# Moving eight weight sums of a fused attention and MLP kernel from GpSimd to VectorE

## The chip, the cores and the metric

One core of one Trainium2 chip. The metric is the device time of one execution in microseconds; times below are medians of all runs. A single core's run counts as slow when it is over 1.5% above the fastest of the same kernel, and ratios and means use fast runs alone; the slow ones are named where they fall. A ratio is the mean time of one kernel's fast runs over the mean of the other's fast runs in the same rounds, so it is not quite the ratio of the medians quoted beside it.

Engine names in the profile: PE is TensorE's matmuls, PEld its weight loads, DVE is VectorE, ACT is ScalarE, POOL is GpSimd. "L276" is line 276 of the kernel's file. The granted clock is the share of TensorE's full clock that its throttle let through. An eviction is the VectorE or ScalarE instruction that empties a PSUM bank. A V group is a run of 28 matmuls of the sigmoid scores with v.

## The reference, cut to what matters

```python
# q, k, v: (8, 12, 448, 64); w_in: (768, 2048); w_out: (2048, 768); all float32
scores = q @ k.T / sqrt(64) - log(448)
attn   = sigmoid(scores) @ v                # no softmax: a plain sigmoid
x      = attn, heads side by side: (3584, 768)
h      = x @ w_in
out    = (h * sigmoid(h)) @ w_out
```

The kernel works in float16 and multiplies by w_out with a Strassen-like scheme: w_out and the activations are cut into quarters, seven products replace eight, and sums of quarters are needed on both sides.

## The kernel before

Everything is put in order on the host by a planner (`Plan`), which models when each engine is free and emits each instruction when its time comes. On the chip the engines run their queues in that order and wait for each other by semaphores.

Loads are issued from GpSimd's queue:

```python
def load(key, deps, fn, nd, size):
    first = [("issue", pl.loads)] if pl.loads else []
    pl.loads += 1
    pl.op("POOL", 650, key, deps + first, fn, nbytes=...)
```

Elementwise operations go to VectorE (`tt`) or GpSimd (`tt_pool`). The quarter sums of w_out are made once, in two halves of four sums each, 1536 columns a sum, all on GpSimd:

```python
def tt(key, dur, deps, o, a, b_, op, prio=0):
    pl.op("DVE", dur, key, deps, lambda: nc.vector.tensor_tensor(o, a, b_, op), prio=prio)      # L276

def tt_pool(key, n, deps, o, a, b_, op, prio=0):
    pl.op("POOL", 100 + 2.2 * n, key, deps, lambda: nc.gpsimd.tensor_tensor(o, a, b_, op), prio=prio)  # L279

def sums_wo(f0, f1):                                # called for (0, 4) and (4, 8)
    ...
    for z, (o, x_, y_) in enumerate(((t1, a12, a11), (t2, a22, t1), (a12, a22, a12), (t4, a21, t2))):
        dz = dep if z == 0 else [kk + (z - 1,)]
        if z in (0,1,2,3):
            tt_pool(kk + (z,), (f1 - f0) * HE, dz, o, x_, y_, sub, 5)
        else:
            tt(kk + (z,), d, dz, o, x_, y_, sub, 5)
```

The matching sums of the activations, 1024 columns each and four for each of 14 row blocks, are on VectorE. They all go through `tt`, so the profile has them at line 276:

```python
# G2.sums
tt(kk + (1,), 600, self.deps + old(0), s1, a21, a22, add, -1)
tt(kk + (2,), 600, [kk + (1,)] + old(1), s2, s1, a11, sub, -1)
tt(kk + (3,), 600, [kk + (2,), kk + (1,)], a21, a11, a21, sub, -1)
tt(kk + (4,), 600, [kk + (2,)] + old(2), s4, a12, s2, sub, -1)
```

VectorE also empties PSUM. The silu multiply (line 624 of the kernel before) reads a PSUM bank and the sigmoid that ScalarE made of it, and frees the bank:

```python
pl.op("ACT", 50 + ncol / 1.2, key + ("sg",), dep,
      lambda: nc.scalar.activation(t[:, :ncol], src_, AF.Sigmoid, scale=ISX), prio=0)
pl.op("DVE", 65 + ncol / 0.96, key + ("g",), [key + ("sg",)] + list(guard),
      lambda: nc.vector.tensor_tensor(o, src_..., t[:, :ncol]..., ALU.mult))
```

There are eight banks, and TensorE stops when all of them wait to be emptied.

## Time and profile before

| | kernel before |
|---|---|
| time, median of 3 runs | 400.0 us (399.7 to 401.24) |
| TensorE busy | 94% of the span |
| VectorE, ScalarE, GpSimd busy | 53%, 58%, 23% |
| GpSimd's eight sums | 25.1 us |

TensorE is the bound. In a kernel like this the thing to read is not the busy shares but the few places where TensorE is not busy, or busy at a lower clock: the row of 40 slices shows where, the list of waits shows for whom, and the timeline of the engine that was waited for shows why. The prediction below prints those lines, and they are not repeated here.

### The profile page before, as it was taken

The numbers are of one execution on the slowest core, as the hardware profiler recorded it, in microseconds if no ns is written. First come the engines' busy times: TensorE is split into PE (matmuls) and PEld (weight loads), VectorE is DVE, ScalarE is ACT, GpSimd is POOL, SyncE is SP. The second block draws the span as 40 slices with busy tenths as digits, with TensorE's granted clock in tenths as the row PEclk, the third lists the DMA queues.
The fourth block names the chain that finished last, engine by engine and source line by source line (L and its number), as shares of the span: only waits on it lengthen the run. The fifth ranks groups of instructions, "written<-read, shape, count | busy, mean of one in ns | idle before, by whom it ended". The sixth has DMA issues, their size and how long they took to land.

```text
span 400.2 us, 17994 instructions
## 1 busy us (share of the span) xinstructions
PE 375.7 (94%) x8024; PEld 315.7 (79%) x8024; DVE 211.1 (53%) x368; ACT 232.8 (58%) x506; POOL 90.1 (23%) x105
## 2 busy tenths in 40 slices
PE   7999869995999999969999999999999999999995
PEld 3676757893887889958898889887989888988773
DVE  4536694797326447415365254554554545554633
ACT  2994629625787686445955697658647766134110
POOL 9656461892222202202022012220200000000000
PEclk9999968997999999998999999999999999999998
DMA  8999990990599996866688999988875101310235
GB/s 111 200 209 203 211 167 2 139 146 2 72 143 196 214 169 104 118 148 121 71 137 107 185 148 130 140 127 116 131 125 115 24 2 43 82 44 2 52 73 120
DMA packets 80636, 46.51 MB, mean 116 GB/s; under 512 B 50608, under 2 KB 79792, under 8 KB 80560
## 3 DMA queue, kind: packets, MB, share of 16 engines
q0 software_dynamic: 25008, 22.81, 38.4%
q1 hardware_dynamic: 55552, 22.56, 33.7%
q8 instruction: 63, 1.03, 1.0%
q14 instruction: 13, 0.11, 0.1%
HBM read 45.61 MB, written 11.01 MB: 141 GB/s over the span
## 4 chain that ended last, share of the span: by engine, by line
PE 82%; DMA 6%; DVE 5%; ACT 3%; issue 2%; POOL 0%; ACTq 0%; DVEq 0%; POOLq 0%
PE ps L803 31%; PE ps L677 29%; PE ps L502 8%; PE ps L514 8%; PE ps L713 5%; DMA xk<-in_k_dram 5%; DVE gs L276 2%; ACT at L952 2%; DVE gt L624 1%; DMA xq<-in_q_dram 1%; PE ps L985 1%; ACT sg L619 1%; PE ps L460 1%; DVE kT L474 1%; ACT at L545 0%
## 5 line engine op out<-in xcount | busy, mean ns | idle before, releaser
L677 PE MATMUL ps<-xt,wi 64*64 64x448 f16 x2304 | 166.9, 352 | 4.1 <-issue 3.7
L545 ACT ACTIVATE at<-ps 128x448 f16<-128x448 f32 x252 | 122.3, 553 | 50.8 <-PE ps L502 43.3
L677 PEld LDWEIGHTS <-wi 64*64 64x64 f16 x2304 | 114.7, 108 | 17.4 <-issue 6.1
L624 DVE TENSOR_TENSOR gt<-ps,sg 128x448 f16<-128x448 f32 (+2 forms) x128 | 78.0, 621 | 76.6 <-ACT sg L619 76.5
L803 PE MATMUL ps<-wo,gt 64*64 64x384 f16 x1344 | 114.9, 326 | 3.3 <-DVE gt L624 3.3
L803 PEld LDWEIGHTS <-gt 64*64 64x64 f16 x1792 | 98.9, 108 | 15.6 <-issue 5.9
L619 ACT ACTIVATE sg<-ps 128x448 f16<-128x448 f32 (+2 forms) x128 | 69.8, 552 | 63.9 <-PE ps L677 32.6
L803 PEld LDWEIGHTS <-gs 64*64 64x64 f16 x1344 | 78.9, 108 | 8.8 <-issue 0.7
L803 PE MATMUL ps<-so,gs 64*64 64x384 f16 x896 | 83.0, 326 | 0.0
L502 PE MATMUL ps<-qT,kT 64*64 64x448 f16 (+2 forms) x840 | 80.4, 334 | 2.2 <-DVE gt L624 1.1
L817 DVE SCALAR_TENSOR_TENSOR us<-ps,us 128x384 f32<-128x384 f32 x70 | 38.8, 555 | 56.7 <-PE ps L803 46.7
L239 POOL DMA_DIRECT2D v<-in_v_dram x24 | 17.4, 724 | 194.2 <-PE ps L514 77.8
L502 PEld LDWEIGHTS <-kT 64*64 64x64 f16 x840 | 37.5, 112 | 12.7 <-issue 8.1
L952 ACT ACTIVATE at<-ps 128x512 f16<-128x512 f32 (+3 forms) x96 | 39.6, 543 | 10.8 <-PE ps L502 10.7
L803 PE MATMUL ps<-so,gt 64*64 64x384 f16 x448 | 44.6, 323 | 0.1
L514 PE MATMUL ps<-at,v 64*64 64x448 f16 (+2 forms) x840 | 42.1, 322 | 2.7 <-DMA xk<-in_k_dram 1.5
L713 PE MATMUL ps<-xt,wi 128*128 128x256 f16 (+1 forms) x384 | 42.8, 268 | 1.4 <-issue 1.1
L803 PE MATMUL ps<-wo,gs 64*64 64x384 f16 x448 | 43.7, 323 | 0.0
L713 PEld LDWEIGHTS <-wi 128*128 128x128 f16 x384 | 34.8, 101 | 6.6 <-issue 2.8
L514 PEld LDWEIGHTS <-v 64*64 64x64 f16 x840 | 30.9, 110 | 7.3 <-issue 3.6
L824 ACT ACTIVATE us<-ps 128x384 f32<-128x384 f32 x28 | 14.0, 501 | 30.3 <-PE ps L803 30.3
L557 DVE TENSOR_SCALAR xt<-ps 128x448 f16<-128x448 f32 x36 | 20.9, 619 | 17.8 <-PE ps L514 16.2
(33 smaller groups left out, 183.8 us busy)
## 6 DMA issues: line engine op xcount, KB each, us to landing
out_dram<-us SPq DMA_DIRECT2D x112, 96.0 KB, 3.1
xk<-in_k_dram POOLq DMA_DIRECT2D x24, 224.0 KB, 6.2
v<-in_v_dram POOLq DMA_DIRECT2D x24, 224.0 KB, 5.2
xq<-in_q_dram POOLq DMA_DIRECT2D x21, 224.0 KB, 7.3
wo<-in_moe_w_out_dram POOLq DMA_DIRECT2D x4, 768.0 KB, 15.3
wi<-in_moe_w_in_dram POOLq DMA_DIRECT2D x8, 192.0 KB, 7.1
wi<-in_moe_w_in_dram POOLq DMA_DIRECT2D x4, 384.0 KB, 9.5
qT<-xq SPq DMA_TRANSPOSE x32, 4.7
```

What stands on the lines that cost most here:

```text
L239: lambda: nc.gpsimd.dma_start(v16[n % NV], src(v, b, g)),
L502: nc.tensor.matmul(pt[r][64 * h : 64 * h + 64, lo : lo + (c1 - c0) * D], kT[n % NTR][64 * r : 64 * r + 64, i, 64 * h : 64 * h + 64], qT[n ...
L514: nc.tensor.matmul(pt[h][64 * j : 64 * j + 64, :N], v16[n % NV][64 * h : 64 * h + 64, j, c * D : (c + 1) * D], at[64 * h : 64 * h + 64, sl ...
L545: lambda r=r: nc.scalar.activation(at[:, sl, r], pt[r][:, :S], AF.Sigmoid, bias=NEG_LOG_S, scale=QKSCALE),
L557: lambda h=h: nc.vector.tensor_scalar_mul(x[:, 2 * g + h, :], pt[h][:, :S], SX), prio=-2,
L619: lambda: nc.scalar.activation(t[:, :ncol], src_, AF.Sigmoid, scale=ISX), prio=0,
L624: lambda: nc.vector.tensor_tensor(o, src_.rearrange("p (a t) -> p a t", a=nb), t[:, :ncol].rearrange("p (a t) -> p a t", a=nb), ALU.mult),
L677: nc.tensor.matmul(bank[64 * j : 64 * j + 64, z * N : z * N + N], wi[64 * h : 64 * h + 64, cc, f0 + 64 * j : f0 + 64 * j + 64], x[64 * h : ...
L713: nc.tensor.matmul(bank[:, z * N : z * N + N], wi[:, cc, fc * P : (fc + 1) * P], x[:, cc, self.c0 : self.c1], start=(cc == 0 and z == 0), ...
L803: nc.tensor.matmul(bank[64 * j : 64 * j + 64, :HE], lhs[64 * h : 64 * h + 64, c, 64 * j : 64 * j + 64], rhs[64 * h : 64 * h + 64, c, :], s ...
L817: lambda: nc.vector.scalar_tensor_tensor(o, bank[:, :HE], ISX, u, ALU.mult, ALU.add), prio=-2,
L952: lambda r=r, src_=src_: nc.scalar.activation(at[:, base : base + m, r, :N], src_, AF.Sigmoid, bias=NEG_LOG_S, scale=QKSCALE),
```

## The change

The intent: give the eight w_out sums to VectorE, which has room on average, and keep everything else.

```diff
+    last_load = [None]
     def load(key, deps, fn, nd, size):
         first = [("issue", pl.loads)] if pl.loads else []
+        if key[0] in ("k", "q", "v") and key[1] >= 99:
+            first.append(last_load[0])
+        last_load[0] = key
...
-            if z in (0,1,2,3):
+            if z in ():
                 tt_pool(kk + (z,), (f1 - f0) * HE, dz, o, x_, y_, sub, 5)
             else:
                 tt(kk + (z,), d, dz, o, x_, y_, sub, 5)
```

The edit of `load` has no effect, because attention groups are numbered 0 to 23. All lines from there on move down by five: 276 becomes 281, 624 becomes 629, 803 becomes 808.

## The prediction

> **What bounds the kernel now.** I read the page's busy shares and its 40 slices first, then what TensorE (PE) waits for, then the VectorE (DVE) and GpSimd (POOL) timelines around the two slices where PE drops. From the page's first two parts:
>
> ```profile
> PE 375.7 (94%) x8024; PEld 315.7 (79%) x8024; DVE 211.1 (53%) x368; ACT 232.8 (58%) x506; POOL 90.1 (23%) x105
> ...
> PE   7999869995999999969999999999999999999995
> ...
> PEclk9999968997999999998999999999999999999998
> ```
>
> PE is 94% busy, so only its holes and its slow-clock stretches can be won. One slice is 10 us. Holes stand in slices 50-60, 90-100 and 170-180 us, and the granted clock falls in or right after each. The waits of PE between 30 and 110 us name the first two (columns: engine, line, what it waited for, us in total, times, longest):
>
> ```profile
> PE ps L803 <- DVE gt L624: 3.3, 1, 3.3
> PE ps L460 <- DVE gt L624: 2.3, 1, 2.3
> PE ps L514 <- DMA xk<-in_k_dram: 1.5, 1, 1.5
> PE ps L502 <- DVE gt L624: 1.1, 2, 0.6
> ```
>
> Line 624 is the silu multiply on VectorE that empties a PSUM bank. Why is it late, when VectorE is only 53% busy? Its timeline and GpSimd's (start, duration, engine, line):
>
> ```profile
> 47.92 1.57 DVE L276 TENSOR_TENSOR gs<-gt 128x1024 f16<-128x1024 f16 x1
> ...
> 49.87 3.44 DVE L276 TENSOR_TENSOR gs<-gs,gt 128x1024 f16<-128x1024 f16 x1
> ...
> 53.71 3.11 DVE L276 TENSOR_TENSOR gt<-gt 128x1024 f16<-128x1024 f16 x1
> 56.74 0.68 DVE L276 TENSOR_TENSOR gs<-gt,gs 128x1024 f16<-128x1024 f16 x1
> ...
> 83.72 9.30 DVE L276 TENSOR_TENSOR gs<-gt 128x1024 f16<-128x1024 f16 x1
> ```
>
> ```profile
> 45.85 3.08 POOL L279 TENSOR_TENSOR so<-wo 128x1536 f16<-128x1536 f16 x1 [4.81 <-DMA wo<-in_moe_w_out_dram]
> 49.68 3.09 POOL L279 TENSOR_TENSOR so<-wo,so 128x1536 f16<-128x1536 f16 x1 [0.75 <-DMA wo<-in_moe_w_out_dram]
> 52.72 3.54 POOL L279 TENSOR_TENSOR wo<-wo 128x1536 f16<-128x1536 f16 x1
> ...
> 80.24 6.16 POOL L279 TENSOR_TENSOR so<-wo,so 128x1536 f16<-128x1536 f16 x2
> 86.35 3.09 POOL L279 TENSOR_TENSOR wo<-wo 128x1536 f16<-128x1536 f16 x1
> 89.39 3.07 POOL L279 TENSOR_TENSOR so<-wo,so 128x1536 f16<-128x1536 f16 x1
> ```
>
> The same VectorE sum takes 0.68 us or up to 9.30 us. Every long one ends about 0.56 us after a GpSimd sum ends: GpSimd 48.93, VectorE 49.49; 52.77 and 53.31; 56.26 and 56.82; 92.46 and 93.02. So the long durations are blocking, not work. In the last case VectorE was passed over by four GpSimd sums in a row.
>
> The 1.5 us put down to a DMA I read differently. That matmul (57.94) writes a bank which the program order makes wait for a line 624 multiply, and that multiply ends at 57.88. It is the same stall.
>
> **What the Trainium skill says.** "SBUF — State Buffer", section "Who interferes with whom": a VectorE instruction with two SBUF inputs contends with a GpSimd instruction that reads SBUF, and the later one blocks for the whole instruction. The pairs above agree. "VectorE: DVE Perf Modes", the errata section, gives (N+151)/0.96 ns for a two-input op; the tier table gives such ops 2x on 16-bit data. With N/2 for N = 1024 that is 690 ns; the trace has 676 to 693 ns unblocked. "GPSIMD Engine Reference", section 4.1, calls GpSimd about 2x slower for two inputs. This trace has 3.09 us per 1536 columns there against my 0.96 us below, so 3.2x. "TensorE: Matmul & The Clock Gate", Part 1: about 3.4 us of idleness halves the clock. After the holes the trace has 0.67 (50-60 us) and 0.72 (90-100 us), and matmuls of 192 columns in groups of twelve take 2.10 instead of 1.16 us.
>
> **The change, part by part.**
>
> Removed: eight GpSimd sums, 4 x 3095 + 2 x 3314 + 2 x 3094 ns = 25.1 us. GpSimd is 23% busy, so that time itself is worth nothing.
>
> Removed with it: the VectorE blocking. First stall (1.57 + 3.44 + 3.11) - 3 x 0.68 = 6.1 us; second 9.30 - 0.68 = 8.6 us. Together 14.7 us of VectorE.
>
> Added: eight VectorE sums of 1536 columns. Estimate from the skill's form above, whose slope the trace confirms: (768+151)/0.96 = 957 ns, so 7.7 us in all. VectorE's net load falls by 7 us.
>
> Moved: the built program has the same 16,050 rows on PE, in another order from row 2169 on (the host-side planner sees other times). The eight sums sit in VectorE's queue among the multiplies and evictions: six between about the 60 and 69 us positions of the old trace, one each later. The load edit tests for a number of 99 or more; attention groups are numbered 0 to 23, so it does nothing.
>
> Worth on PE, first stall. I redo the VectorE chain by hand with 0.68 us sums. The sum of 49.87 then ends near 50.3, the multiply waiting on ScalarE (ACT) runs 51.5-52.0, two sums end near 53.3, the next multiply near 53.8. So the matmul group of 57.94 starts near 53.9: 4.1 us won, and PE idles about 0.7 instead of 3.8 us, too little for the clock to fall. The slow clock after the old stall (about 2.6 us from 57.94 to 63) mostly stays hidden: ScalarE is 9.05 of 10 us busy in 60-70 and runs one queue of evictions from 60.15 to 67.9. I count 0.8 us of it. So 4.9 us before the new work. Then four of the added sums come before the evictions that the matmuls of old time 66.40 need. By the same chain the eviction comes near 62.4, where ScalarE would have let PE start near 61.2: minus 1.2 us. **Net first stall: about 3.7 us.**
>
> Second stall. PE idles 3.35 + 0.55 + 0.54 = 4.4 us (its timeline at 93.55, 94.61 and 95.68). From 93.55 to 101.0 it is at half rate: four matmuls start per 0.33 us where 0.165 is normal later. That is 7.45 - 1.09 of waits = 6.4 us at half rate, so 3.2 us lost. Before it PE is 10.00 of 10 us busy (80-90), and after it 10.00 of 10 (100-110), so nothing else hides this gain. **Second stall: about 7.6 us.**
>
> Sum 11.3 us; 400.0 - 11.3 = 388.7. I take **389 us**.
>
> **The rivals.**
>
> 1. VectorE becomes the bound where the six sums crowd. Between 60 and 70 us it has 4.1 us of work, and six sums add 5.7 us into an interval that itself shrinks: nearly full, with in-order evictions behind 1 to 2 us of sums. For it: these are the stages where PE borrows banks from evictions. Against: the old VectorE sat idle 2.1, 1.6, 1.9 and 1.2 us there, and the planner places the sums at lowest priority. If it bites fully, the first stall gives back all its 3.7 us and the result is 392 to 393.
>
> 2. The hole is hidden anyway: ScalarE or the w_out and K/V loads pace 45-70 us. For it: DMA runs near 210 GB/s until 58 us and ScalarE's 9.05 of 10. Against: all weight pieces lie in SBUF before VectorE reaches the sums (GpSimd saw the first two at 45.85 and 49.68; they leave at about 3.8 us each, so the last comes near 57.5, and VectorE needs it near 63). This costs only the first stall again.
>
> 3. The later program is another order with other luck. One hole at 175.64 lasts 3.06 us with every engine idle and no releaser ("issue"), and runs cold for some us after. I do not know its cause; if it is an accident of timing it may vanish (minus 4 us) or another may come (plus 4 us).
>
> 4. GpSimd's loads starve behind VectorE sums, since it must write descriptors. The skill's page infers that two-input ops spare the write side. Loads are far ahead of use after 60 us, so I give it 1 us at most.
>
> **Range and chances.** Both stalls are plain in the trace and their cause ends the moment GpSimd stops reading SBUF; that gives 11.3 us as centre. Rival 1 takes up to 4, rival 3 is plus or minus 4, and a fuller recovery of the slow clock in the first stall gives up to 2 more. So 383 to 394. Faster by 2% needs under 392.0: it fails only if rival 1 bites fully or a new hole comes, 0.79. Within 2% 0.20, slower 0.01.
>
> **What would show it.** Right: line 276 sums all near 0.68 us, with none over 1.2; eight new sums near 0.96 us each; no PE wait on line 624 over 1 us between 80 and 100 us and no fall of the clock there; VectorE busy down by about 7 us to near 204; PE busy down by 4 to 6 us to near 370, as cold matmuls vanish; GpSimd busy near 65. Wrong: PE waits on VectorE of 1 to 3 us between 55 and 75 us (rival 1); unchanged evictions but holes marked issue or DMA elsewhere (rival 3); sums that still last over 1.2 us, which would mean the blocker was the GpSimd DMA issues and not its sums.

## The result, and the profile after

| | before | after |
|---|---|---|
| median | 400.62 us (4 runs, 399.7 to 403.27) | 385.81 us (4 runs, 385.25 to 387.09) |
| ratio of fast runs | | 0.9624, 95% interval 0.957 to 0.9679 |

It is faster by 3.8%, 14.8 us by the medians. The predicted time was 389 us and the predicted gain 11.3 us.

The page of the kernel after, busy shares, then TensorE's row of slices and its granted clock (one slice is now 9.6 us):

```profile
PE 366.5 (95%) x8024; PEld 307.8 (80%) x8024; DVE 203.5 (53%) x376; ACT 232.6 (60%) x506; POOL 65.1 (17%) x97
...
PE   7899899999998899989999999999999999999994
...
PEclk9999999999999999999999999999999999999998
```

The 6 and the 5 of the two holes are gone, and the clock stays in the top tenth in every slice but the last. TensorE's busy time fell by 9.2 us for the same 8024 matmuls. That fits matmuls that had run at a lower clock: a group of twelve that took 2.10 us in the first stall takes 1.16 or 1.17 us now.

What TensorE waited for between 30 and 110 us in the kernel after (line, what for, us in total, times, longest):

```profile
PE ps L718 <- issue: 1.1, 1, 1.1
PE ps L507 <- issue: 0.4, 1, 0.4
PE ps L507 <- ACT at L957: 0.3, 1, 0.3
```

No wait for VectorE is left. VectorE's timeline after (start, duration, engine, line, operation), with the sums that correspond to those of 1.57, 3.44, 3.11 and 9.30 us before:

```profile
47.35 0.68 DVE L281 TENSOR_TENSOR gs<-gt 128x1024 f16<-128x1024 f16 x1
...
48.41 0.68 DVE L281 TENSOR_TENSOR gs<-gs,gt 128x1024 f16<-128x1024 f16 x1
...
49.48 0.68 DVE L281 TENSOR_TENSOR gt<-gt 128x1024 f16<-128x1024 f16 x1
...
54.47 0.95 DVE L281 TENSOR_TENSOR so<-wo 128x1536 f16<-128x1536 f16 x1
55.45 0.96 DVE L281 TENSOR_TENSOR so<-wo,so 128x1536 f16<-128x1536 f16 x1
...
76.71 0.69 DVE L281 TENSOR_TENSOR gs<-gt 128x1024 f16<-128x1024 f16 x1
```

Each old sum takes its own 0.68 to 0.69 us, and the new ones 0.95 us. Two stretches of the two kernels side by side, first before and then after. The columns are the stretch in us, its length, the busy time of PE, PEld, DVE, ACT and POOL with instruction counts, the granted clock, the DMA share and GB/s:

```profile
50.00:60.00 10.00, 6.20 (x99) 5.32 (x100) 10.00 (x10) 2.98 (x8) 6.26 (x2) 0.67 0.96 169
90.00:100.00 10.00, 5.56 (x48) 3.24 (x49) 7.95 (x11) 5.12 (x11) 2.47 (x1) 0.72 0.01 2
```

```profile
50.00:60.00 10.00, 9.40 (x199) 7.32 (x196) 9.68 (x19) 8.77 (x23) 0.00 (x0) 1.00 1.00 176
90.00:100.00 10.00, 10.00 (x236) 8.47 (x230) 3.52 (x6) 8.33 (x20) 2.15 (x3) 1.00 1.05 164
```

VectorE is 10.00 us "busy" before with 10 instructions and 9.68 us after with 19. A blocked instruction counts as busy, which is why the shares alone did not give the stall away.

Where the time came from can be read off by following the same pieces of work through both TensorE timelines:

| piece of TensorE's work | before, us | after, us | lead |
|---|---|---|---|
| V group ahead of the first stall | 46.25 | 45.68 | 0.57 |
| V group held up in the first stall | 57.94 | 52.31 | 5.63 |
| first w_in matmuls of the second batch | 66.40 | 59.77 | 6.63 |
| run of 132 w_in matmuls begins | 78.18 | 71.16 | 7.02 |
| first product with w_out | 93.55 | 83.12 | 10.43 |
| first V group of 448 columns | 105.24 | 90.50 | 14.74 |
| end | 400.2 | 384.5 | 15.7 |

The first row is scatter between executions, since nothing differs up to there. The first stall gives 7.02 - 0.57 = 6.45 us, the second 14.74 - 7.02 = 7.72 us, and the 295 us after it 1.0 us. That last 1.0 us is a net of larger terms, which no part of the change was meant to give: the 2000th matmul starts 15.1 us earlier than before (at 117.2 us before), the 3000th only 11.2 us (163.6) and the 4000th again 14.7 us (213.3). Short holes in TensorE's work took the time, and an older hole that is gone gave it back (see rival 3 below). That they nearly cancel is luck.

One reading of the page could now be checked. The wait of the matmuls of 57.94 had been put down to the landing of a K load, 19.0 us after its issue at 39.15. That is near 58.2, after they had started. In the kernel after that load takes 18.9 us from 39.88 and lands near 58.8, long after the same matmuls have started at 52.31. They never needed it.

### The profile page after: what moved, and what is told of

Its sections match the earlier page's. It is cut to its first block, busy times and chain, and to the rows that moved or that the text cites. A ratio compares the mean times of both kernels' runs of the same rounds, so it can differ in the third digit from the quotient of the medians.

```text
span 384.5 us, 17994 instructions
## 1 busy us (share of the span) xinstructions
PE 366.5 (95%) x8024; PEld 307.8 (80%) x8024; DVE 203.5 (53%) x376; ACT 232.6 (60%) x506; POOL 65.1 (17%) x97
## 4 chain that ended last, share of the span: by engine, by line
PE 90%; issue 3%; ACT 2%; DMA 2%; POOL 1%; DVE 1%; POOLq 0%; ACTq 0%
PE ps L808 33%; PE ps L682 30%; PE ps L718 10%; PE ps L507 8%; PE ps L519 8%; ACT at L957 2%; DMA xk<-in_k_dram 2%; PE ps L465 1%; PE ps L990 1%; POOL xk L224 0%; POOL xq L233 0%; DVE qT L479 0%; DVE xt L979 0%; ACT sg L624 0%; POOL v L244 0%
## 5 line engine op out<-in xcount | busy, mean ns | idle before, releaser
L682 PEld LDWEIGHTS <-wi 64*64 64x64 f16 x2304 | 112.6, 107 | 19.3 <-issue 7.0
L808 PE MATMUL ps<-wo,gt 64*64 64x384 f16 x1344 | 111.5, 323 | 0.3 <-issue 0.3
L808 PEld LDWEIGHTS <-gt 64*64 64x64 f16 x1792 | 97.8, 107 | 10.7 <-issue 1.9
L808 PE MATMUL ps<-so,gs 64*64 64x384 f16 x896 | 80.6, 323 | 0.0
L507 PE MATMUL ps<-qT,kT 64*64 64x448 f16 (+2 forms) x840 | 76.5, 318 | 2.2 <-ACT at L957 0.9
L507 PEld LDWEIGHTS <-kT 64*64 64x64 f16 x840 | 35.7, 108 | 11.9 <-issue 7.8
L718 PE MATMUL ps<-xt,wi 128*128 128x256 f16 (+1 forms) x384 | 40.8, 260 | 1.1 <-issue 1.1
L519 PE MATMUL ps<-at,v 64*64 64x448 f16 (+2 forms) x840 | 40.9, 313 | 0.6 <-issue 0.6
L718 PEld LDWEIGHTS <-wi 128*128 128x128 f16 x384 | 33.1, 98 | 5.8 <-issue 2.5
L519 PEld LDWEIGHTS <-v 64*64 64x64 f16 x840 | 29.8, 107 | 6.2 <-issue 2.2
```

The lines of the kernel that those rows point to most:

```text
L507: nc.tensor.matmul(pt[r][64 * h : 64 * h + 64, lo : lo + (c1 - c0) * D], kT[n % NTR][64 * r : 64 * r + 64, i, 64 * h : 64 * h + 64], qT[n ...
L519: nc.tensor.matmul(pt[h][64 * j : 64 * j + 64, :N], v16[n % NV][64 * h : 64 * h + 64, j, c * D : (c + 1) * D], at[64 * h : 64 * h + 64, sl ...
L682: nc.tensor.matmul(bank[64 * j : 64 * j + 64, z * N : z * N + N], wi[64 * h : 64 * h + 64, cc, f0 + 64 * j : f0 + 64 * j + 64], x[64 * h : ...
L718: nc.tensor.matmul(bank[:, z * N : z * N + N], wi[:, cc, fc * P : (fc + 1) * P], x[:, cc, self.c0 : self.c1], start=(cc == 0 and z == 0), ...
L808: nc.tensor.matmul(bank[64 * j : 64 * j + 64, :HE], lhs[64 * h : 64 * h + 64, c, 64 * j : 64 * j + 64], rhs[64 * h : 64 * h + 64, c, :], s ...
```

## The experiments

The theory: a GpSimd operation that reads SBUF blocks a VectorE operation with two SBUF inputs, and the VectorE queue behind it holds PSUM banks. Rivals: the planner's new program order made the gain; GpSimd's sums or the loads queued behind them came too late; any GpSimd work on SBUF blocks. All kernels gave correct results, on two chips: e1 to e4 on one and the rest on another. "Before" is the kernel before, run beside them. All runs were fast but one of e5's four (397.91 us) and one of the kernel before in each of the two later batches (408.39 and 406.19 us).

| run | what it does | median, us | ratio to before (95%) |
|---|---|---|---|
| e1_order_before | sums on VectorE, TensorE's order of before | 383.93 | 0.959 (0.954 to 0.964) |
| e2_order_after | sums on GpSimd, TensorE's order of after | 395.27 | 0.985 (0.980 to 0.991) |
| e3_dummy_read | e1 plus eight useless GpSimd subtractions | 405.56 | 1.010 (1.005 to 1.016) |
| e4_dummy_write | e1 plus sixteen useless GpSimd memsets | 384.92 | 0.960 (0.956 to 0.964) |
| e5_first_on_gpsimd | only the first half's sums on GpSimd | 394.54 | 0.980 (0.970 to 0.989) |
| e6_second_on_gpsimd | only the second half's sums on GpSimd | 393.03 | 0.980 (0.974 to 0.986) |
| e7_sums_apart | all on GpSimd, VectorE's sums moved away | 386.89 | 0.964 (0.956 to 0.973) |
| e8_after_beside | the kernel after | 388.57 | 0.969 (0.962 to 0.975) |
| f1_order_before | e1 again | 387.10 | 0.968 (0.964 to 0.972) |
| f2_after | the kernel after again | 386.00 | 0.966 (0.961 to 0.971) |
| f3_first_on_gpsimd | e5 again | 393.15 | 0.984 (0.978 to 0.989) |
| f4_second_clean | e6 with one sum moved | 389.28 | 0.974 (0.969 to 0.979) |

Held to 2%, e1, e4, e7, e8, f1, f2 and f4 are faster than the kernel before and e3 is the same. e2, e5, e6 and f3 are unclear: their intervals lie below 1, but it is not settled whether they gain 2%.

### Order against engine: e1 and e2

e1 leaves the planner believing that the sums are GpSimd's, and issues them on VectorE. The built TensorE, ScalarE and store queues have the same instructions in the same order as before.

```diff
 def tt_pool(key, n, deps, o, a, b_, op, prio=0):
-    pl.op("POOL", 100 + 2.2 * n, key, deps, lambda: nc.gpsimd.tensor_tensor(o, a, b_, op), prio=prio)
+    pl.op("POOL", 100 + 2.2 * n, key, deps, lambda: nc.vector.tensor_tensor(o, a, b_, op), prio=prio)
```

> The eight sums run on VectorE, but the planner still counts them as GpSimd's, so TensorE, ScalarE and the store queue keep exactly the order of the kernel before. Theory (GpSimd's reading sums blocked VectorE's two-input sums): the gain stays, 385 to 389 us, every 1024-column sum of line 276 at 0.68 to 0.70 us. Rival (the new program order made the gain): about 400 us.

e2 is the converse: planned as VectorE's, issued on GpSimd.

```diff
-                tt(kk + (z,), d, dz, o, x_, y_, sub, 5)
+                pl.op("DVE", d, kk + (z,), dz, lambda o=o, x_=x_, y_=y_: nc.gpsimd.tensor_tensor(o, x_, y_, sub), prio=5)
```

> The program order of the kernel after on TensorE, but the eight sums on GpSimd, six of them back to back from about 46 us. Theory: the first stall stays or grows, since the sums of line 276 at 47 to 51 us are blocked again, and the second goes, since GpSimd is done with its sums before 77 us: 390 to 396 us. Rival (order): 386 us.

Measured: e1 383.93 us, a little below its range, with every sum of line 276 at 0.68 to 0.69 us; e2 395.27 us. e1 has the whole gain in the order of before, so the gain follows the engine and not the order. e2 keeps about a third of it. The first sums of the row blocks, 14 of them, in the kernel before and then in e1 (shortest, median and longest in ns):

```profile
L276 DVE TENSOR_TENSOR gs<-gt x14: 683/691/9304, 47.9 to 371.8; 128x1024 f16<-128x1024 f16 x14
L276 DVE TENSOR_TENSOR gs<-gt x14: 682/691/693, 47.4 to 352.5; 128x1024 f16<-128x1024 f16 x14
```

In e2 six GpSimd sums run from 47.44 to 68 us, and VectorE's timeline shows all four sums of the first block blocked:

```profile
48.10 2.97 DVE L281 TENSOR_TENSOR gs<-gt 128x1024 f16<-128x1024 f16 x1
50.99 0.55 DVE L629 TENSOR_TENSOR gt<-ps,sg 128x384 f16<-128x384 f32 x1
51.46 3.45 DVE L281 TENSOR_TENSOR gs<-gs,gt 128x1024 f16<-128x1024 f16 x1
...
55.30 3.10 DVE L281 TENSOR_TENSOR gt<-gt 128x1024 f16<-128x1024 f16 x1
58.33 3.56 DVE L281 TENSOR_TENSOR gs<-gt,gs 128x1024 f16<-128x1024 f16 x1
```

The multiply, whose first input is PSUM, takes its usual 0.55 us; it is late only because it stands behind a blocked sum. The second block's sums, at 88 to 91 us, come after GpSimd's last sum (84.07) and take 0.68 us: as expected, one stall grew and the other went.

### Blocking against lateness, reading against writing: e3 and e4

Both start from e1 and add work on GpSimd whose result nobody reads, where the kernel before had its sums. TensorE's order is again that of before.

```diff
+    dum = sb("dum", [4, HE], F16)
...
-                tt_pool(kk + (z,), (f1 - f0) * HE, dz, o, x_, y_, sub, 5)
+                def both(o=o, x_=x_, y_=y_, z=z):
+                    nc.vector.tensor_tensor(o, x_, y_, sub)
+                    nc.gpsimd.tensor_tensor(dum, a11, a11 if z == 0 else a21, sub)    # e3
+                    # e4 instead: nc.gpsimd.memset(dum, 0.0) twice
+                pl.op("POOL", 100 + 2.2 * (f1 - f0) * HE, kk + (z,), dz, both, prio=5)
```

> As e1, plus eight GpSimd subtractions of the same size on data that nobody uses, at the places where the kernel before had its sums. They read SBUF and nobody waits for them. Theory: the blocking is back, line 276 again up to 3 and 9 us for one sum, the new sums of 0.95 us are blocked as well: 398 to 406 us. Rival (the time went to waiting for GpSimd's results, not to blocking): 385 to 389 us as e1.

> As e3, but each dummy subtraction is two GpSimd memsets of the same tile, which write SBUF and read nothing. Theory (it is the read side that is shared): no blocking, all sums of line 276 near 0.69 us, 385 to 389 us. Rival A (any GpSimd work on SBUF blocks VectorE): several of these sums over 1.2 us and 392 us or more. Rival B (the K/V loads queued behind GpSimd's work cost the time): slower than e1 by 3 us or more, with no sum long.

Measured: e3 405.56 us, e4 384.92 us. In e3 nobody waits for GpSimd's results, and the whole loss is back and 1.0% more (0.5% to 1.6%). Its VectorE timeline:

```profile
50.85 3.11 DVE L277 TENSOR_TENSOR gt<-gt 128x1024 f16<-128x1024 f16 x1
53.88 3.56 DVE L277 TENSOR_TENSOR gs<-gt,gs 128x1024 f16<-128x1024 f16 x1
```

VectorE's own w_out sums are blocked as well: two of them, at 81.54 and 88.74, take 3.78 and 3.84 us instead of 0.95. No sum reached the 9 us that I had expected. This trace is level with the kernel before at its first product with w_out (93.10 against 93.55 us) and 2.7 us behind at the first V group of 448 columns (107.98 against 105.24). Between them TensorE waits 2.98 us for a multiply behind the sum of 88.74 and another of 3.10 us at 92.97. In e4 VectorE's and GpSimd's timelines overlap and nothing is long:

```profile
47.86 0.68 DVE L277 TENSOR_TENSOR gs<-gt 128x1024 f16<-128x1024 f16 x1
48.46 0.55 DVE L629 TENSOR_TENSOR gt<-ps,sg 128x384 f16<-128x384 f32 x1
48.93 0.68 DVE L277 TENSOR_TENSOR gs<-gs,gt 128x1024 f16<-128x1024 f16 x1
```

```profile
47.71 1.38 POOL L295 MEMSET dum<- 128x1536 f16 x1
49.14 1.38 POOL L296 MEMSET dum<- 128x1536 f16 x1
```

Seven more two-input sums run beside the memsets of 74.34 to 85.80 us, none longer than its own 0.68 to 0.95 us. A memset writes SBUF and reads nothing, so the conflict is with GpSimd's reads. "SBUF — State Buffer", section "Who interferes with whom", says just this of two-input VectorE operations, and these two runs agree with it. A GpSimd operation with a single SBUF input was not tried. e4 also clears the loads: they stand behind 22.1 us of memsets there, and nothing is lost.

### GpSimd as the place, without the overlap: e7

All eight sums stay on GpSimd, but the planner must put VectorE's sums of the first two row blocks behind them.

```diff
+            apart = swo_all if pi < 2 else []
-            tt(kk + (1,), 600, self.deps + old(0), s1, a21, a22, add, -1)
+            tt(kk + (1,), 600, self.deps + old(0) + apart, s1, a21, a22, add, -1)
```

> All eight sums stay on GpSimd, but VectorE's two-input sums of the first two blocks are put behind them in VectorE's order, so that the two kinds hardly overlap. Theory (blocking, not where the work is done): 383 to 389 us, with at most one sum of line 276 over 1.2 us. Rival (GpSimd is too slow a place for these sums): 394 us or more.

Measured: 386.89 us, with the kernel after at 388.57 us in the same rounds. The intervals overlap, so neither is the faster. (The new dependency also gives the other engines a third order, whose own worth is not separated here.) One sum of the pair below was still caught, by GpSimd's last sum (82.65 to 85.75 us), and TensorE did not wait for it:

```profile
83.18 3.73 DVE L276 TENSOR_TENSOR gs<-gt 128x1024 f16<-128x1024 f16 x2
```

GpSimd is three times slower at these sums, and here that costs nothing. What cost time was when they ran.

### The size of each stall: e5, e6, f1 to f4

Planner and TensorE's order are those of before; only the issuing engine differs by half.

```diff
-                tt_pool(kk + (z,), (f1 - f0) * HE, dz, o, x_, y_, sub, 5)
+                eng = nc.gpsimd if f0 == 0 else nc.vector        # e5; e6 has f0 != 0
+                pl.op("POOL", 100 + 2.2 * (f1 - f0) * HE, kk + (z,), dz,
+                      lambda eng=eng, o=o, x_=x_, y_=y_: eng.tensor_tensor(o, x_, y_, sub), prio=5)
```

> TensorE's order as before; the four sums of the first half of w_out stay on GpSimd, the four of the second half go to VectorE. Only the first stall (about 48 to 57 us) should be left. My prediction valued it at 3.7 us, the two traces side by side at about 6.5 us. By the prediction: 387 to 389 us; by the traces: 389.5 to 392 us.

> The other way round: only the four sums of the second half stay on GpSimd, so only the second stall should be left, one sum of line 276 long. Valued at 7.6 us by the prediction, at about 8 us by the traces: 390.5 to 393 us. If the two stalls are independent, what this kernel and the one with the first half lose against e1 (383.9) adds up to the whole 16 us; if one hides part of the other, the sum is different by more than 2 us.

> The kernel after again, on the chip of the halves, so that their differences can be read on one chip: 384 to 387 us.

Measured: 394.54 (393.7 without its slow run), 393.03 and 388.57 us. e5 came above both of its ranges, e8 above its own and e6 at the edge of its own. In this batch the kernel after took 2.8 us more than when the prediction was tested; in the next one, on the same chip, it took 386.00 us (f2), so that is scatter between batches and not shown to be the chip. The ranges had been drawn from e1, which was not run in this batch, and the test whether e5's and e6's losses add up to 16 us cannot be read. e6 also blocked something else than intended: the first half's fourth sum, now VectorE's, stands late in the queue and met GpSimd's chain.

```profile
74.36 10.06 DVE L293 TENSOR_TENSOR so<-wo,so 128x1536 f16<-128x1536 f16 x1
```

So I repeated e5 beside e1 on one chip with five rounds, and mended e6: in f4 the first half's fourth sum is issued on VectorE right behind its third.

```diff
+                def put(z=z, o=o, x_=x_, y_=y_):
+                    if f0:
+                        nc.gpsimd.tensor_tensor(o, x_, y_, sub)
+                    elif z < 3:
+                        nc.vector.tensor_tensor(o, x_, y_, sub)
+                    if not f0 and z == 2:
+                        nc.vector.tensor_tensor(t4, a21, t2, sub)
```

> The same kernel as e1, as the common foot of the three beside it: about 384 us. If the program order of the kernel before is really the better one, it beats the kernel after by 1 to 2 us here too; if that was the chip, the two are within 1 us.

> The kernel after on the same chip as f1, to compare the two orders: 385 to 388 us.

> Only the first stall left, TensorE's order as in f1. The prediction's 3.7 us puts it at f1 plus 3 to 4.5 us, the traces' 6.5 us at f1 plus 5.5 to 8 us.

> Only the second half on GpSimd, as in e6, but the first half's last sum is issued on VectorE right behind its third, so that GpSimd can block only a sum of line 276. One such sum over 5 us; f1 plus 7 to 9 us. With f3 the two losses should add up to the loss of the kernel before (about 16 us) within 2 us, if the stalls are independent.

Means of the fast runs: before 400.2, f1 387.4, f2 386.5, f3 393.5, f4 389.8 us. From their scatter, a difference of two of them is good to about 2 us (95%). f1 came 3 us above the 384 that was expected from e1.

- **Order.** f1 and f2 differ by 0.9 us, the other way round than e1 (383.93) and the kernel after (385.81) in the earlier batches. The order is worth nothing that these runs can show.
- **First stall.** f3 - f1 = 6.1 us. That agrees with the traces' 6.5 us and is only just clear of the prediction's 3.7 us.
- **Second stall.** before - f3 = 6.7 us, with the first stall present in both. The prediction said 7.6.
- **f4 missed.** It loses 2.4 us against f1, where 7 to 9 were expected, and f3's and f4's losses add up to 8.5 of 12.8 us.

f4's VectorE and TensorE timelines suggest why the last two differ (this is read from traces; no run changes the chain's length alone). The kept trace is of the slowest of f4's six runs, 393.36 us:

```profile
78.06 6.27 DVE L276 TENSOR_TENSOR gs<-gt 128x1024 f16<-128x1024 f16 x1
```

```profile
75.80 8.74 PE L720 MATMUL ps<-xt,wi 128*128 128x256 f16 x102
84.86 0.51 PE L810 MATMUL ps<-wo,gt 64*64 64x384 f16 x4 [0.32 <-DVE gt L631]
85.92 0.35 PE L509 MATMUL ps<-qT,kT 64*64 64x448 f16 x1 [0.55 <-DVE gt L631]
86.99 0.38 PE L509 MATMUL ps<-qT,kT 64*64 64x448 f16 x3 [0.72 <-DVE gt L631]
```

The sum is blocked until the end of GpSimd's chain of sums in both kernels, but the chain is shorter here. Before, the first half's fourth sum had been stuck behind loads in GpSimd's queue and ran directly ahead of the second half's last three: a chain of four from 80.24 us, and 9.30 us of blocking. In f4 it is three from 74.58 us, and 6.27 us. In both, VectorE's sum came 3.48 us after the chain's start, when its first sum was over. TensorE has some 6.5 us of queued matmuls to run while VectorE is blocked (from 83.72 to 90.2 us before, from 78.06 to 84.5 us here). Only what VectorE is late by after that, with the 0.55 us multiply behind the sum, costs time: 4.4 us of idleness before, 0.32 + 0.55 + 0.72 = 1.6 us here. With a clock of 0.63 over the following 88 to 92 us, which is about 4 x 0.37 = 1.5 us, f4's stall comes to some 3 us by this estimate, against 2.4 in the means. The loss is not proportional to the blocking, and the halves cannot be added.

## Why the prediction was right, point by point

- **The cause.** Right, and now shown: e1 excludes the order and e2 agrees, e3 brings the loss back without anybody waiting for GpSimd, e4 shows that it takes a read.
- **The cost of the added work.** Right: 957 ns a sum estimated, 0.95 us measured; VectorE 204 us busy predicted, 203.5 measured; GpSimd 65 and 65.1. (The terms for the eight GpSimd sums add to 25.2 us, not 25.1.)
- **The second stall.** 7.6 us predicted, 7.7 us in the two traces, 6.7 us in the means of before and f3. One reading under it was wrong: VectorE was not "passed over by four GpSimd sums in a row". The first of the four had ended near 83.3 us when VectorE's sum started at 83.72; it waited out three and was passed over twice. The value came from TensorE's timeline and does not rest on it.
- **The first stall: the mis-sized term.** "Net first stall: about 3.7 us"; it measured 6.1 us (f3 - f1) and 6.45 us (traces). Two steps of it failed.
  - "The multiply waiting on ScalarE (ACT) runs 51.5-52.0": I had paired the multiply with a later sigmoid, that of 50.91 us; its own had ended at 46.91. In the kernel after it runs 49.01 to 49.56, so the matmul group that was to start near 53.9 starts at 52.31, or 52.9 with the 0.57 us that this execution was ahead: 1.0 us more.
  - "Minus 1.2 us" for the added sums in front of the evictions: the matmuls of old time 66.40 were to start near 62.4 and start at 59.77 (60.3 with the same shift). After the first step's 1.0 us there remain 1.1 us, nearly the whole charge. The two steps explain 2.1 of the 2.4 to 2.75 us that were missing. VectorE is 9.68 of 10 us busy in 50-60 us and 9.08 in 60-70, as rival 1 feared, but no wait of TensorE on it is left: the sums fell where the evictions had slack.
- **The clock.** TensorE's busy time was to fall by 4 to 6 us and fell by 9.2. I held the slow clock after the first stall to be hidden by ScalarE's queue; but that queue also starts 6.6 us earlier, its run of four evictions at 53.53 instead of 60.15.
- **The rivals.** Rival 1 did not bite. Rival 2: TensorE waits 0.3 us for ScalarE between 30 and 110 us, and all its waits of the kind in the profile after come to 0.9 us. Rival 3: both of its cases came, and nearly cancelled. The 3.06 us hole near 175 us is not in the profile after, whose longest "issue" wait is 1.7 us; but such waits on the w_in matmuls add up to 4.9 us, against 3.7 before, and 3.9 us of them lie between 110 and 150 us. Holes of 0.5 to 3.8 us stand between 109 and 183 us in the trace of every kernel here, in e1's once (0.86 us) and in e3's twice (3.82 and 1.12 us). What causes them stays open, and a single trace can be off by 2 to 4 us through them. Rival 4: no sign of it, and e4's loads bore a longer queue than these.

No version beats the kernel after for certain: e1 was at 0.959 and e7 at 0.964 of before, but f1 was at 0.968 beside f2's 0.966, all with overlapping intervals.

## What to carry to other kernels

An engine that is half idle on average can still be the one that stops TensorE, if single instructions of it are blocked: look at the longest instruction of a group against its shortest (0.68 against 9.30 us here) before believing busy shares. Work "moved off" VectorE to GpSimd is not off it when GpSimd reads SBUF while VectorE works on two SBUF inputs; put it on VectorE if its own time is short, or run it when VectorE has no two-input work, as e7 did. And count what a stall costs from the end of the queued work, not from its beginning: 9.3 us of blocking cost about 7 us, 6.3 us about 2.4 to 3.

## What the Trainium skill lacked or had wrong

- "SBUF — State Buffer", section "Who interferes with whom", says that whoever issues first gets the shared ports for the whole instruction. It does not say who is next when GpSimd's operations follow each other without a gap. In e2 VectorE got in at every boundary (blocked 2.97, 3.45, 3.10, 3.56 us), and three of the GpSimd sums that followed took 3.53 to 3.54 us instead of 3.09, so GpSimd was held up in its turn. In the kernel before it was passed over at two boundaries (9.30 us), and in e6 it waited out three sums (10.06 us), though its own start is recorded 0.04 us ahead of the first (74.36 against 74.40; GpSimd's times are rough). What decides is open.
- The same section gives no duration for a VectorE sum that is let in. In the kernel before, a 1024-column sum ends 0.54 to 0.56 us after the GpSimd operation does, less than its own 0.68 us, as if about 0.13 us of it were already over when it is blocked.
- "GPSIMD Engine Reference", section 4.1, calls GpSimd about 2x slower for two inputs. The page's measured table, in section 3.1, is for fp32. In float16 a 1536-column subtraction took 3.09 us there and 0.95 us on VectorE: 3.3x.
- "TensorE: Matmul & The Clock Gate", Part 1, lowers the clock after a window of about 3.4 us of idleness. In the kernel before a single gap of 2.33 us was enough: the clock is 0.85 over 52-54 us and 0.50 over 54-56, before the next gap. In f4 gaps of 0.32, 0.55 and 0.72 us, with TensorE busy for 2.29 of the 4 us from 84, were followed by 0.63 over 88-92 us. The page's section "A second HAM failure mode: psum-queue depth-cycling" has short idle times between groups of matmuls do this too, but gives no length for them.
